# Attention products of two token tiles as one six-bank unit instead of one tile in four banks

## The chip, the cores and the metric

One core of a Trainium2 chip runs the whole kernel. The metric is the device time of one execution in microseconds, taken as the median of several executions. All executions used here were in the fast state, with the full clock granted to TensorE (0.999 to 1.0). Executions of one kernel scatter by about 0.5 us to either side.

The engines are named as the profile names them: PE is TensorE (PEld its weight loads), DVE is VectorE, ACT is ScalarE, POOL is GpSimd, SP is SyncE.

## The reference, cut to what matters

```python
# x: 1 x 2048 x 640, 32 heads of 20, F = 1536, bf16
xn = layernorm(x)
q, k, v = heads(xn @ wqkv)
phi_q = concat(softmax(q @ w_phi), softmax(-(q @ w_phi)))     # per head, 40 features
phi_k = concat(softmax(k @ w_phi), softmax(-(k @ w_phi)))
kv, z = einsum(phi_k, v), sum(phi_k)                          # over all tokens
o = (phi_q @ kv) / (phi_q @ z + 1e-6)
out = x + o @ wo + (silu(xn @ w1) * (xn @ w3)) @ w2
```

There are 16 token tiles of 128 tokens. The change concerns `phi_q @ kv` with its two denominators for each tile, and nothing else in the mathematics.

## The kernel before: the parts that matter

The kernel describes its work as units: a unit is a run of matmuls together with the PSUM banks that it fills (PSUM is the memory into which matmuls write) and the DVE and ACT operations that read them out. A list scheduler, which runs when the program is built, puts the units in an order on PE, gives each its banks out of eight, and orders the operations on every engine, from modelled durations. Near-ties are decided by pseudo-random tolerances drawn from `SEED`. So another seed gives another order of much the same instructions.

Four kinds of unit fill the second part of the program: Q units (`q_proj`, one bank, 5 matmuls of 512 columns, then two exponentials on ACT), gated units (`mlp`, two banks, 10 of 512), output units (`out_tile`, two banks, 34 of 320), and attention units:

```python
def q_tok(t, level):                      # one token tile; called 16 times
    u = P.begin(4, level, "row", "qt")    # four banks
    for sg in range(2):                   # exp(+) and exp(-)
        for c in range(DC):               # 5 groups of 4 heads (22 columns per head)
            for r in range(2):            # the two 64-row halves of the PE array
                j = 2 * sg + r
                mm(j, lambda k, j=j, c=c: bank(k + j, 88, 66 * c),
                   EqT[...][64 * r:64 * r + 64, sg, c, ...], KVc[64 * r:64 * r + 64, sg, c, :], ...)
    # ACT: two copies of the denominators out of PSUM into e_s, 64 each
    # DVE: pr = e * e', den = pr0 + pr1, 1/den, g = e' / den   (64, 32, 32, 64 elements)
    # DVE: prod = PSUM * g, 1280 elements, the last reader of all four banks
    # DVE: o = prod0 + prod1, then a DMA transpose into oT for the output unit
```

These matmuls contract over 64 rows, two of them side by side in the halves of the array; every other unit of this part uses the full 128 rows. So PE changes its mode on entering an attention unit and again on leaving it. The bank choice in the scheduler tries the places in order (cuts marked):

```python
for u in sorted(ready_u, key=lambda u: (-u.level, u.mms[0].idx)):
    ...
    for k in range(0, 8, u.banks) if u.anchor is None else ():
        ...
        g = group_time(u, k)              # when the banks' last readers are modelled to end
```

The program's first part, the front, normalises x, transposes it, computes K and V, and folds `w_phi` into the projections (units `fold0.0` to `fold0.4` make `Wqp`, the folded Q weights). It ends with a unit named `kvback`, which sets up `KVc`; the attention part follows.

The softmax here doesn't subtract the row's maximum and nothing guards it: scores larger than these inputs give would overflow.

Of the kernel before, what the change touches and what calls it, by code (L numbers as in the profile page):

```python
# [4 lines left out]
ACT = mybir.ActivationFunctionType  # L5
# [50 lines left out]
class _Unit:  # L56


    def __init__(self, banks, level, mode):
        self.banks, self.level, self.mode, self.k = banks, level, mode, None  # L60
        self.mms = []
        self.first = {}
        self.readers = [[] for _ in range(banks)]
        self.behind = []
        self.anchor = None
        self.name = ""


class _Program:
# [102 lines left out]
    def schedule(self, start, filler=None, filler_until=0.0, seed=None, shaken=0.0):  # L172
# [39 lines left out]
        mode = "full"  # L212
# [118 lines left out]

        def fit(k, n, t):

            if n == 4:
                return 0
            size = 2 * n
            base = k // size * size
            return sum(1 for i in range(base, base + size) if not k <= i < k + n and bank_time(i, 0.0, True) <= t)
# [3 lines left out]
        while left:  # L342
            best = None
            pick = None
            if ready_u:
# [7 lines left out]
                for u in sorted(ready_u, key=lambda u: (-u.level, u.mms[0].idx)):  # L353
                    opts = [(u.at, 0, u.anchor.k)] if u.anchor is not None else []
                    for k in range(0, 8, u.banks) if u.anchor is None else ():
                        if blocked & set(range(k, k + u.banks)):
                            continue
                        g = group_time(u, k)
                        if g < 1e8:
                            opts.append((max(g, u.at), fit(k, u.banks, u.at), k))  # L360
# [4 lines left out]
                    if u.banks == 4 and u.at <= t0 + 1.0 and not blocked and (not opts or x[0] > u.at + 0.03):  # L365
                        k = min((group_time(u, k, True), k) for k in (0, 4))[1]
                        blocked |= set(range(k, k + 4))
# [23 lines left out]
            if e == "PE":  # L391
# [25 lines left out]
                mode = x.mode  # L417
# [79 lines left out]
SEED = 1138  # L497
# [3 lines left out]
def bass_parallel_sum__linear_kernel_hedgehog__glu_gated_swiglu__prompt_kernel(  # L501
# [43 lines left out]
    pr_s = new("pr_s", [128, 2, 2, H], f32)  # L545
    den_s = new("den_s", [128, 2, H], f32)
    g_s = new("g_s", [128, 2, 2, H], f32)
# [37 lines left out]
    e_s = new("e_s", [128, 2, 4, H], f32, RV + 20480)  # L585
# [4 lines left out]
    prod = new("prod", [128, 2, 2, D], bf, RW + 1760)  # L590
# [411 lines left out]
    def q_tok(t, level):  # L1002
        b, jj = divmod(t, 4)
        u = P.begin(4, level, "row", "qt")
        u.name = f"qt{t}"
        u.behind.extend(turned[-1:])
        for sg in range(2):
            for c in range(DC):
                for r in range(2):
                    j = 2 * sg + r  # L1010
                    mm(j, lambda k, j=j, c=c: bank(k + j, 88, 66 * c),
                       EqT[b % 2][64 * r:64 * r + 64, sg, c, 128 * jj:128 * jj + 128],
                       KVc[64 * r:64 * r + 64, sg, c, :], c == 0, c == DC - 1, True,
                       0.003 if r == 0 else 0.045)

        def ps(k):
            a = PS[:, k * 512:(k + 4) * 512].rearrange("p (n c) -> p n c", c=512)[:, :, 0:352]
            return a.rearrange("p n (h c) -> p n h c", c=22)
        e = e_s[:, t % 2, :, :]
        up = 2e6  # L1020
        for sg in range(2):
            o = e[:, sg:4 - sg:3 - 2 * sg, :]
            add([w_act(o.rearrange("p c (q h) -> p q h c", h=16),
                       lambda k, sg=sg: ps(k)[:, 2 * sg:2 * sg + 2, :, 20:22], ACT.Copy, 64)],
                [e], [], [2 * sg, 2 * sg + 1], up)
        pr, den, g = pr_s[:, t % 2, :, :], den_s[:, t % 2, :], g_s[:, t % 2, :, :]
        add([w_tt("DVE", pr, e[:, 0:2, :], e[:, 2:4, :], ALU.mult, 64)], [pr], [e], None, up)
        add([w_tt("DVE", den, pr[:, 0, :], pr[:, 1, :], ALU.add, 32)], [den], [pr], None, up)
        add([w_op("DVE", "reciprocal", (den, den), 0.27, 0.36)], [den], [den], None, up)
        add([w_tt("DVE", g, e[:, 2:4, :], den.unsqueeze(1).to_broadcast([128, 2, 32]), ALU.mult, 64)],  # L1030
            [g], [e, den], None, up)
        gq = g.rearrange("p s (q h) -> p (s q) h", h=16)
        p2 = prod[:, t % 2, :, :]
        add([w_tt("DVE", p2.rearrange("p s (q h c) -> p (s q) h c", q=2, c=DH), lambda k: ps(k)[:, :, :, 0:DH],
                  gq.unsqueeze(3).to_broadcast([128, 4, 16, DH]), ALU.mult, 1280)],
            [p2], [g], [0, 1, 2, 3], up)
        turned.append(P.all[-1])
        o = o_tok[:, t % 4, :]
        add([w_tt("DVE", o, p2[:, 0, :], p2[:, 1, :], ALU.add, D, 2)], [o], [p2], None, 5e5)
        turn(oT[:, :, t * 128:(t + 1) * 128], o, 1e5 - t)  # L1040
# [21 lines left out]
    def out_tile(t, level):  # L1062
        b, ti = divmod(t, 4)
        u = P.begin(2, level, stream="O")
        u.name = f"O{t}"
        chunks = [(hT[b][:, i, ti * 128:(ti + 1) * 128], w2_s, i) for i in range(FC)]
# [139 lines left out]
    for b in range(NB):  # L1206
        for j in range(4):
            t = 4 * b + j
            q_tok(t, when(110 + t))
            if b + 1 < NB:  # L1210
                for fc in range((5 * j + 3) // 4, (5 * j + 8) // 4):
                    q_proj(b + 1, fc, when(110 + t + 0.1 * fc))
# [65 lines left out]
```

## Time and profile before

| | before |
|---|---|
| device time, median of 3 runs | 274.07 us (273.82 to 274.29) |
| span of the profiled execution | 271.7 us |
| DVE, ACT busy | 182.5 us, 101.8 us |
| from the first V matmul on the transposed tiles (`PS<-wv,xnT`) to the first matmul after `kvback` | 98.97 us |
| from there to the start of the last matmul | 157.92 us |

The span is the time between the first and last instruction of the profile; it is about 2 us shorter than the device time. The last two rows are differences of start times of matmuls in the trace. I shall call them the **middle** and the **attention part**. What lies ahead of the middle, some 12 us of loading and normalising the first token tiles and of early V matmuls on them, I call the **start**. Times between the starts of successive matmuls I call steps; a matmul is late by what its step is longer than usual for its shape. Some traces lack a few matmul records, and a step over a missing one is no wait. The lines of the page on which the argument stands are quoted in the prediction, those of a timeline with start in us, duration, engine, line, operation, operands, count. These are lines of the timeline of all engines before (start in us, duration, engine, line, operation, operands, count):

```profile
66.27 1.47 DVE L627 TENSOR_REDUCE S<-ekt 128x64 f32<-128x1280 bf16 x1
...
66.92 0.79 PE L619 MATMUL PS<-BDc,wqkT 128*128 128x140 bf16 x12
...
67.65 0.88 DVE L627 CAST Wqp<-PS 128x320 bf16<-128x320 f32 x2
68.31 0.77 ACT L627 ACTIVATE Wqp<-PS 128x320 bf16<-128x320 f32 x2
...
68.91 0.48 PE L619 MATMUL PS<-BDc,wqkT 128*128 128x140 bf16 x6
69.22 1.11 PE L619 MATMUL PS<-Wkp,xnT 128*128 128x320 bf16 x7
```

Two fold units (12 matmuls) start at 66.92. Behind a reduction (`S`) DVE makes two of the four copies that read them out of PSUM, until 68.53, and ACT the other two, until 69.08. The next fold unit, `fold0.3` (6 matmuls), starts at 68.91 and runs without a gap.

### The profile page before, as it was taken

How to read it: one execution, taken by the hardware profiler on the slowest of the kernel's cores; microseconds unless marked ns; L12 is line 12 of the kernel's file. 1: busy time of each engine (PE TensorE's matmuls, PEld its weight loads, DVE VectorE, ACT ScalarE, POOL GpSimd, SP SyncE). 2: the span in 40 equal slices, each digit the busy share in tenths (PEclk: the TensorE clock that was granted, in tenths of full speed). 3: DMA queues.
4: the chain of work that ended last, by engine and by line, in shares of the span. 5: the costliest groups of instructions: out<-in, count | busy, mean ns of one | idle time of the engine just before them, and what ended most of it. 6: DMA issues, size and time to landing. Idle time of an engine off the chain costs nothing.

```text
span 271.7 us, 5074 instructions
## 1 busy us (share of the span) xinstructions
PE 268.3 (99%) x2098; PEld 159.4 (59%) x2098; DVE 182.5 (67%) x325; ACT 101.8 (37%) x190; POOL 60.8 (22%) x101
## 2 busy tenths in 40 slices
PE   8999999999999999999999999999999999999996
PEld 5746546777754448444444446777677774444774
DVE  5758989999998453688869994777673215666112
ACT  6436726777744531355583354100100002222000
POOL 4320642789999900000000000000000000000000
PEclk9999999999999999999999999999999999999999
DMA  7657996763000001703041111333643122000001
GB/s 224 200 112 241 355 186 127 113 169 123 0 0 2 0 0 17 278 0 51 0 51 24 24 27 33 91 97 100 94 102 91 58 79 67 0 0 0 27 24 48
DMA packets 39975, 21.98 MB, mean 81 GB/s; under 512 B 27024, under 2 KB 39952, under 8 KB 39952
## 3 DMA queue, kind: packets, MB, share of 16 engines
q1 hardware_dynamic: 39376, 21.01, 31.8%
q10 hardware_dynamic: 576, 0.66, 0.7%
q8 instruction: 16, 0.26, 0.4%
q14 instruction: 7, 0.06, 0.1%
HBM read 12.81 MB, written 2.62 MB: 57 GB/s over the span
## 4 chain that ended last, share of the span: by engine, by line
PE 99%; DVE 0%; issue 0%
PE PS L619 96%; PE PS L1098 2%; PE PS L867 0%; PE PS L814 0%; DVE xres L627 0%
## 5 line engine op out<-in xcount | busy, mean ns | idle before, releaser
L619 PE MATMUL PS<-xnT,w_s 128*128 128x512 bf16 x480 | 106.6, 379 | 0.0
L619 PEld LDWEIGHTS PS<-xnT,w_s 128*128 128x128 bf16 x480 | 46.5, 98 | 54.7
L627 ACT ACTIVATE th<-PS 128x512 f32<-128x512 f32 x48 | 28.7, 597 | 71.9 <-PE PS L619 71.8
L619 PE MATMUL PS<-w_s,hT 128*128 128x320 bf16 (+2 forms) x384 | 55.0, 299 | 0.0
L627 DVE SCALAR_TENSOR_TENSOR t<-th,PS 128x512 bf16<-128x512 f32 x48 | 32.7, 683 | 27.5 <-ACT th L627 27.5
L619 PEld LDWEIGHTS PS<-w_s,hT 128*128 128x128 bf16 x384 | 37.0, 98 | 14.9
L627 POOL TENSOR_TENSOR ekt<-ekt,rS 128x640 bf16<-128x640 bf16 x32 | 39.4, 1269 | 1.1 <-DVE rS L627 1.1
L627 DVE TENSOR_TENSOR xres<-PS,xres 128x640 bf16<-128x640 f32 (+2 forms) x17 | 13.4, 786 | 37.8 <-PE PS L619 37.8
L627 DVE SCALAR_TENSOR_TENSOR hT<-t,PS 128x512 bf16<-128x512 bf16 x48 | 32.7, 684 | 1.3
L627 ACT ACTIVATE EqT<-PS 128x512 bf16<-128x512 f32 x40 | 21.9, 594 | 11.8 <-PE PS L619 11.7
L619 PE MATMUL PS<-wo_s,oT 128*128 128x320 bf16 (+2 forms) x160 | 24.5, 299 | 0.0
L627 DVE TENSOR_TENSOR prod<-PS,g_s 128x1280 bf16<-128x1280 f32 x16 | 23.9, 1491 | 0.6
L627 ACT ACTIVATE ekt<-PS 128x640 bf16<-128x640 f32 x32 | 20.8, 701 | 9.0 <-PE PS L619 8.8
L619 PE MATMUL PS<-Wkp,xnT 128*128 128x320 bf16 x160 | 23.9, 299 | 0.0
L619 PE MATMUL PS<-xnT,Wqp 128*128 128x512 bf16 x100 | 23.4, 380 | 0.0
L627 ACT ACTIVATE e_s<-PS 128x64 f32<-128x64 f32 x32 | 9.0, 283 | 38.2 <-PE PS L619 37.7
L627 DVE TENSOR_REDUCE S<-ekt 128x64 f32<-128x1280 bf16 x16 | 22.9, 1447 | 0.0
L619 PE MATMUL PS<-wv,xnT 128*128 128x320 bf16 x130 | 19.8, 299 | 0.0
L619 PEld LDWEIGHTS PS<-wo_s,oT 128*128 128x128 bf16 x160 | 15.7, 98 | 6.1
L619 PEld LDWEIGHTS PS<-Wkp,xnT 128*128 128x128 bf16 x160 | 15.5, 98 | 5.9
L619 PEld LDWEIGHTS PS<-xnT,Wqp 128*128 128x128 bf16 x100 | 9.4, 98 | 11.0
L627 DVE BATCH_NORM_STATS2 bst<-x_tok 128x6 f32<-128x320 bf16 x32 | 14.1, 469 | 2.4 <-DMA x_tok<-in_A_x_dram 2.4
(66 smaller groups left out, 163.3 us busy)
## 6 DMA issues: line engine op xcount, KB each, us to landing
w_s<-in_B_w_dram SPq DMA_DIRECT2D x6, 640.0 KB, 7.6
xres<-in_A_x_dram SPq DMA_DIRECT2D x16, 160.0 KB, 2.2
out_dram<-xres SPq DMA_DIRECT2D x15, 160.0 KB, 1.8
x_tok<-in_A_x_dram SPq DMA_DIRECT2D x3, 640.0 KB, 8.2
w_s<-in_B_w_dram SPq DMA_DIRECT2D x1, 1920.0 KB, 9.0
wo_s<-in_A_wo_dram SPq DMA_DIRECT2D x1, 800.0 KB, 4.8
x_tok<-in_A_x_dram SPq DMA_DIRECT2D x2, 160.0 KB, 3.4
x_tok<-in_A_x_dram ACTq DMA_DIRECT2D x2, 160.0 KB, 3.8
```

The lines of the kernel that those rows point to most:

```text
L619: return nc.tensor.matmul(o(u.k), l, r, start=start, stop=stop, skip_group_check=shared)
L627: return getattr(e, name)(*[at(a, u) for a in args], **{k: at(v, u) for k, v in kw.items()})
L1098: return nc.tensor.matmul(bank(u.k, n), ones[:, 0:128], ones[:, 0:n], start=True, stop=True)
```

## The change

The intent is to halve the number of mode changes: two tiles of attention run back to back in a unit of six banks. The small DVE and ACT operations are shared between the two tiles (128 or 64 elements at a time instead of 64 or 32), and the read-out product is split in three so that two banks at a time come free. As such a unit leaves only two banks to other work while it is read out, the scheduler is told to prefer a long output unit right behind it. The pseudo-random seed was chosen anew. The diff, cut to its core (cuts marked):

```diff
-                for u in sorted(ready_u, key=lambda u: (-u.level, u.mms[0].idx)):
+                for u in sorted(ready_u, key=lambda u: (-u.level - (1e7 if wide and u.long else 0), u.mms[0].idx)):
                     opts = [(u.at, 0, u.anchor.k)] if u.anchor is not None else []
-                    for k in range(0, 8, u.banks) if u.anchor is None else ():
+                    for k in places(u.banks) if u.anchor is None else ():
 ...
-SEED = 1138
+SEED = 61
 ...
     def q_tok(t, level):
         b, jj = divmod(t, 4)
-        u = P.begin(4, level, "row", "qt")
+        u = P.begin(6, level, "row", "qt")
 ...
         for sg in range(2):
-            for c in range(DC):
-                for r in range(2):
-                    j = 2 * sg + r
+            for m in range(2):
+                for c in range(DC):
+                    parts = ((0, 4),) if not sg or c != 2 else ((0, 1), (1, 4))
+                    for lo, hi in parts:
+                        for r in range(2):
+                            h = 3 * c + lo
+                            j, off = (4 + r, 256 * m + 22 * (h - 7)) if sg and h >= 7 else (2 * r + m, 22 * (16 * sg + h))
 ...
-        add([w_tt("DVE", p2..., lambda k: ps(k)[:, :, :, 0:DH], ..., ALU.mult, 1280)],
-            [p2], [g], [0, 1, 2, 3], up)
+        for r in range(2):
+            add([w_tt("DVE", o, lambda k, r=r: big(k)[:, 2 * r:2 * r + 2, :, 0:DH], ..., ALU.mult, 920)],
+                [o], [i], [2 * r, 2 * r + 1], up)
+        add([w_tt("DVE", o, lambda k: rest(k)[:, :, :, 0:DH], ..., ALU.mult, 720)], [o], [i], [4, 5], up)
 ...
     def out_tile(t, level):
+        u.long = True
 ...
-            q_tok(t, when(110 + t))
+            if j % 2 == 0:
+                q_tok(t, when(118 + 2.5 * t))
```

At one place per tile and sign, four heads straddle the end of a bank, and that matmul is split in one of 22 and one of 66 columns (`parts`).

More of the change, by code (lines that the diff above doesn't have):

```diff
@@ L65, in __init__ @@
         self.anchor = None
+        self.long = False
         self.name = ""
@@ L211, in schedule @@
         queues = {"SP": [], "ACT": []}
-        mode = "full"
+        mode, wide = "full", False
         owner = [None] * 8
@@ L330, in group_time, with places @@
             return max(bank_time(k + j, u.first[j].off if j in u.first else 0.0, guess) for j in range(u.banks))
+        def places(n):
+            return range(0, 9 - n, n if n < 4 else 8 - n)
         def fit(k, n, t):
-            if n == 4:
+            if n >= 4:
                 return 0
@@ L364, in schedule @@
                             pick = (x[0], u, x[2])
-                    if u.banks == 4 and u.at <= t0 + 1.0 and not blocked and (not opts or x[0] > u.at + 0.03):
-                        k = min((group_time(u, k, True), k) for k in (0, 4))[1]
-                        blocked |= set(range(k, k + 4))
+                    if u.banks >= 4 and u.at <= t0 + 1.0 and not blocked and (not opts or x[0] > u.at + 0.03):
+                        k = min((group_time(u, k, True), k) for k in places(u.banks))[1]
+                        blocked |= set(range(k, k + u.banks))
                 if pick is not None:
@@ L416, in schedule @@
                 x.k = k
-                mode = x.mode
+                mode, wide = x.mode, x.banks == 6
                 ready_u.remove(x)
@@ L544, in bass_parallel_sum__linear_kernel_hedgehog__glu_gated_swiglu__prompt_kernel @@
     warm = new("warm", [128, 8], f32)
-    pr_s = new("pr_s", [128, 2, 2, H], f32)
-    den_s = new("den_s", [128, 2, H], f32)
-    g_s = new("g_s", [128, 2, 2, H], f32)
+    pr_s = new("pr_s", [128, 2, 64], f32)
+    den_s = new("den_s", [128, 64], f32)
+    g_s = new("g_s", [128, 4, H], f32)
     S64 = new("S64", [128, 3, 64], f32)
@@ L584, in bass_parallel_sum__linear_kernel_hedgehog__glu_gated_swiglu__prompt_kernel @@
     oT = new("oT", [128, DC, S], bf, RV)
-    e_s = new("e_s", [128, 2, 4, H], f32, RV + 20480)
+    e_s = new("e_s", [128, 4, 64], f32, RV + 20480)
     RW = region(12800)
@@ L589, in bass_parallel_sum__linear_kernel_hedgehog__glu_gated_swiglu__prompt_kernel @@
     KVc = new("KVc", [128, 2, DC, 4 * 22], bf, RW)
-    prod = new("prod", [128, 2, 2, D], bf, RW + 1760)
+    prod = new("prod", [128, 4, H, DH], bf, RW + 1760)
     o_tok = new("o_tok", [128, 4, D], bf, RW + 6880)
@@ L1003, in q_tok @@
         b, jj = divmod(t, 4)
-        u = P.begin(4, level, "row", "qt")
+        u = P.begin(6, level, "row", "qt")
         u.name = f"qt{t}"
         u.behind.extend(turned[-1:])
+        seen = set()
         for sg in range(2):
-            for c in range(DC):
-                for r in range(2):
-                    j = 2 * sg + r
-                    mm(j, lambda k, j=j, c=c: bank(k + j, 88, 66 * c),
-                       EqT[b % 2][64 * r:64 * r + 64, sg, c, 128 * jj:128 * jj + 128],
-                       KVc[64 * r:64 * r + 64, sg, c, :], c == 0, c == DC - 1, True,
-                       0.003 if r == 0 else 0.045)
@@ L1016, in ps @@
-        def ps(k):
-            a = PS[:, k * 512:(k + 4) * 512].rearrange("p (n c) -> p n c", c=512)[:, :, 0:352]
+            for m in range(2):
[5 more added lines that the diff above has]
+                            j, off = (4 + r, 256 * m + 22 * (h - 7)) if sg and h >= 7 else (2 * r + m, 22 * (16 * sg + h))
+                            first = j not in seen
+                            seen.add(j)
+                            n = 22 * (hi - lo)
+                            mm(j, lambda k, j=j, n=n, off=off: bank(k + j, n, off),
+                               EqT[b % 2][64 * r:64 * r + 64, sg, c, 128 * (jj + m):128 * (jj + m) + 128],
+                               KVc[64 * r:64 * r + 64, sg, c, 22 * lo:22 * hi], first,
+                               sg == 1 and (c == 2 and hi == 1 if j < 4 else m == 1 and c == DC - 1), True,
+                               0.003 if r == 0 else max(0.026, 0.008 + n / 2400))
@@ L1018, in ps, with big, rest @@
+        def big(k):
+            a = PS[:, k * 512:(k + 4) * 512].rearrange("p (n c) -> p n c", c=512)[:, :, 0:506]
             return a.rearrange("p n (h c) -> p n h c", c=22)
-        e = e_s[:, t % 2, :, :]
+        def rest(k):
+            a = PS[:, (k + 4) * 512:(k + 6) * 512].rearrange("p (n c) -> p n c", c=256)[:, :, 0:198]
+            return a.rearrange("p n (h c) -> p n h c", c=22)
         up = 2e6
-        for sg in range(2):
-            o = e[:, sg:4 - sg:3 - 2 * sg, :]
-            add([w_act(o.rearrange("p c (q h) -> p q h c", h=16),
-                       lambda k, sg=sg: ps(k)[:, 2 * sg:2 * sg + 2, :, 20:22], ACT.Copy, 64)],
-                [e], [], [2 * sg, 2 * sg + 1], up)
@@ L1026, in q_tok @@
-        pr, den, g = pr_s[:, t % 2, :, :], den_s[:, t % 2, :], g_s[:, t % 2, :, :]
-        add([w_tt("DVE", pr, e[:, 0:2, :], e[:, 2:4, :], ALU.mult, 64)], [pr], [e], None, up)
-        add([w_tt("DVE", den, pr[:, 0, :], pr[:, 1, :], ALU.add, 32)], [den], [pr], None, up)
-        add([w_op("DVE", "reciprocal", (den, den), 0.27, 0.36)], [den], [den], None, up)
-        add([w_tt("DVE", g, e[:, 2:4, :], den.unsqueeze(1).to_broadcast([128, 2, 32]), ALU.mult, 64)],
-            [g], [e, den], None, up)
@@ L1032, in q_tok @@
-        gq = g.rearrange("p s (q h) -> p (s q) h", h=16)
-        p2 = prod[:, t % 2, :, :]
-        add([w_tt("DVE", p2.rearrange("p s (q h c) -> p (s q) h c", q=2, c=DH), lambda k: ps(k)[:, :, :, 0:DH],
-                  gq.unsqueeze(3).to_broadcast([128, 4, 16, DH]), ALU.mult, 1280)],
-            [p2], [g], [0, 1, 2, 3], up)
-        turned.append(P.all[-1])
-        o = o_tok[:, t % 4, :]
-        add([w_tt("DVE", o, p2[:, 0, :], p2[:, 1, :], ALU.add, D, 2)], [o], [p2], None, 5e5)
-        turn(oT[:, :, t * 128:(t + 1) * 128], o, 1e5 - t)
+        e = e_s[:].rearrange("p q (n h) -> p n h q", h=16)
@@ new lines, in q_tok @@
+        for src, o, js in ((lambda k: big(k)[:, :, 0:16, 20:22], e[:, :, :, 0:4:3], [0, 1, 2, 3]),
+                           (lambda k: big(k)[:, :, 16:23, 20:22], e[:, :, 0:7, 1:3], [0, 1, 2, 3]),
+                           (lambda k: rest(k)[:, :, :, 20:22], e[:, :, 7:16, 1:3], [4, 5])):
+            add([w_act(o, src, ACT.Copy, free(o))], [e_s[:]], [], js, up)
+        add([w_tt("DVE", pr_s[:], e_s[:, 0:2, :], e_s[:, 2:4, :], ALU.mult, 128)], [pr_s[:]], [e_s[:]], None, up)
+        add([w_tt("DVE", den_s[:], pr_s[:, 0, :], pr_s[:, 1, :], ALU.add, 64)], [den_s[:]], [pr_s[:]], None, up)
@@ new lines, in q_tok @@
+        add([w_op("DVE", "reciprocal", (den_s[:], den_s[:]), 0.47, 0.56)], [den_s[:]], [den_s[:]], None, up)
+        g = g_s[:].rearrange("p n (s h) -> p s n h", h=16)
+        for sg in range(2):
+            dn = den_s[:].rearrange("p (n h) -> p n h", h=16)
+            add([w_tt("DVE", g[:, sg, :, :], e_s[:, 2 + sg, :].rearrange("p (n h) -> p n h", h=16), dn, ALU.mult, 64)],
+                [g_s[:]], [e_s[:], den_s[:]], None, up)
+        for r in range(2):
+            o, i = prod[:, 2 * r:2 * r + 2, 0:23, :], g_s[:, 2 * r:2 * r + 2, 0:23]
+            add([w_tt("DVE", o, lambda k, r=r: big(k)[:, 2 * r:2 * r + 2, :, 0:DH],
+                      i.unsqueeze(3).to_broadcast([128, 2, 23, DH]), ALU.mult, 920)], [o], [i], [2 * r, 2 * r + 1], up)
@@ new lines, in q_tok @@
+        o, i = prod[:, :, 23:32, :], g_s[:, :, 23:32]
+        add([w_tt("DVE", o, lambda k: rest(k)[:, :, :, 0:DH], i.unsqueeze(3).to_broadcast([128, 4, 9, DH]), ALU.mult,
+                  720)], [o], [i], [4, 5], up)
+        turned.append(P.all[-1])
+        for m in range(2):
+            o = o_tok[:, (t + m) % 4, :]
+            i0, i1 = prod[:, m:4:2, 0:16, :], prod[:, m:4:2, 16:32, :]
+            add([w_tt("DVE", o.rearrange("p (r h c) -> p r h c", r=2, c=DH), i0, i1, ALU.add, D, 2)], [o], [i0, i1],
+                None, 5e5)
+            turn(oT[:, :, (t + m) * 128:(t + m + 1) * 128], o, 1e5 - t - m)
@@ L1208, in bass_parallel_sum__linear_kernel_hedgehog__glu_gated_swiglu__prompt_kernel @@
             t = 4 * b + j
-            q_tok(t, when(110 + t))
+            if j % 2 == 0:
+                q_tok(t, when(118 + 2.5 * t))
             if b + 1 < NB:
                 for fc in range((5 * j + 3) // 4, (5 * j + 8) // 4):
-                    q_proj(b + 1, fc, when(110 + t + 0.1 * fc))
+                    q_proj(b + 1, fc, when(118 + 2.5 * t + 0.1 * fc))
     for t in range(T):
```

## The prediction

> **What bounds the kernel now.** I read the page from the top (busy shares, then the chain that ended last), then the list of waits, then the timeline of TensorE alone, then the trace's start times matmul by matmul.
>
> ```profile
> PE 268.3 (99%) x2098; PEld 159.4 (59%) x2098; DVE 182.5 (67%) x325; ACT 101.8 (37%) x190; POOL 60.8 (22%) x101
> ```
> ```profile
> PE 99%; DVE 0%; issue 0%
> ```
>
> TensorE (PE) is busy for 268.3 of 271.7 us, and the chain is PE from end to end. VectorE and ScalarE have idle time, so making their work shorter gives nothing by itself. What can help is fewer or cheaper PE slots; what can hurt is a wait that PE does not have today. Busy does not mean efficient, so I looked at how far apart the matmuls start. The timeline of PE where output units (24 + 10 matmuls of 320 columns) alternate with attention units (20 of 88 columns), and further down where output units follow each other:
>
> ```profile
> 169.74 0.57 PE L619 MATMUL PS<-KVc,EqT 64*128 64x88 bf16 x20
> 170.24 3.43 PE L619 MATMUL PS<-w_s,hT 128*128 128x320 bf16 x24
> 173.51 1.52 PE L619 MATMUL PS<-wo_s,oT 128*128 128x320 bf16 x10
> 174.97 0.56 PE L619 MATMUL PS<-KVc,EqT 64*128 64x88 bf16 x20
> ...
> 206.20 3.42 PE L619 MATMUL PS<-w_s,hT 128*128 128x320 bf16 x24
> 209.46 1.52 PE L619 MATMUL PS<-wo_s,oT 128*128 128x320 bf16 x10
> 210.82 3.42 PE L619 MATMUL PS<-w_s,hT 128*128 128x320 bf16 x24
> ```
>
> An output unit alone repeats every 210.82 - 206.20 = 4.62 us, which is 34 steps of 136 ns. With an attention unit the period is 174.97 - 169.74 = 5.23 us. One attention unit therefore takes 0.60 us of PE. Single start times split it: the step into the unit is 231 ns where 136 would be normal (95 lost); the step out of it is 134 ns where an 88-column step of 39 would do (95 lost), and the next step is 146 instead of 136 (10 lost). That is 0.20 us for turning the array to 64 rows and back. The rest, 0.40 us, is ten pairs at about 39 ns, plus 8 ns at the start. All 16 units show the same figures, whatever unit stands next to them. From 118 us to the end no other matmul starts late by more than 8 ns: today there is no PSUM wait at all in this part.
>
> **What the Trainium skill says.** "TensorEngine Tiling (Array Packing)", Key Properties: "Mode switching requires drain: Changing tiling mode (not just tile) drains the TensorE". The trace agrees: 95 ns each way, now paid 32 times. "TensorE: Matmul & The Clock Gate", the section "Wait — 56ns, not 53.3ns?": warm matmuls start N/2.4 GHz + about 2.5 ns apart, and never under about 25 ns. The trace agrees (216 ns at 512 columns, 136 at 320, 39 per pair at 88). Its Part 3 says that matmuls in different row groups run together about 4 ns apart; the two halves of a pair start 3 to 4 ns apart here. "PSUM — Partial Sum Buffer", the section on bank collisions: the chip does not stall when an engine reads a bank that PE writes, it reports an error; so PE must wait for the readers, and six banks held by one unit leave two to work in. No wait of that kind is to be seen in this part before.
>
> **The change part by part.**
>
> (1) Removed: 16 attention units become 8, so 8 round trips of 0.20 us go, together with 8 of the 8-ns starts: 8 x 0.209 = 1.67 us.
>
> (2) Added on PE: four bank-crossing chunks are split per unit, giving 44 matmuls (22 pairs) instead of 40. A pair of 88 columns (39 ns) becomes one of 22 (about 27, at the floor) and one of 66 (about 30), twice a unit: 8 x 2 x 18 = 0.29 us. So a wide unit should take 1.03 us against 2 x 0.604. PE saves about 1.4 us before any waits.
>
> (3) VectorE and ScalarE. These rows give their sizes:
>
> ```profile
> L627 DVE TENSOR_TENSOR prod<-PS,g_s 128x1280 bf16<-128x1280 f32 x16 | 23.9, 1491 | 0.6
> L627 DVE RECIPROCAL den_s<-den_s 128x32 f32<-128x32 f32 x16 | 5.6, 353 | 0.5
> L627 DVE TENSOR_TENSOR g_s<-e_s,den_s 128x64 f32<-128x64 f32 x16 | 3.6, 225 | 0.6
> L627 ACT ACTIVATE e_s<-PS 128x64 f32<-128x64 f32 x32 | 9.0, 283 | 38.2 <-PE PS L619 37.7
> ```
>
> At 1.04 ns an element over a fixed 0.16 us, the product of 1280 becomes two of 920 (1.12 us) and one of 720 (0.91). The 64-wide reciprocal takes 0.54 (the same shape stands elsewhere at 536 ns). The DVE chain of a pair is about 4.6 us against 5.0 for two singles. ScalarE does three copies (0.9 us) instead of four (1.13). Neither engine limits, so I credit nothing.
>
> (4) Moved: what the banks allow. By the built program's order the wide units are followed by four Q projections (twice), an output unit (six times); each narrow follower has two banks. Counting from the start of a wide unit: it ends at 0.95, the copies at 2.0, four small DVE steps and the second gain product bring the first product to 3.75, and it ends at 4.87. An output unit holds PE until 5.57, so banks come free in time: **this ordering hides the long read-out**, with some 0.7 us to spare. But three short waits do come up.
> - Q projections in two banks. In the trace a Q unit takes 1.08 us of PE; its first exponential starts 0.416 us after its fifth matmul, the second ends 1.085 us later. Start to bank free is 0.873 + 0.416 + 1.085 = 2.37, plus 0.06 us from a releaser's end to the matmul (DVE to PE at 10.9 us in the trace). The bank is wanted again after 2 x 1.08 = 2.17: PE waits 0.26 us, at two places: 0.53 us.
> - The output unit after the fifth pair takes the bank of a Q unit that ended just before the pair; its exponentials end at 1.19, wanted at 1.10: 0.15 us.
> - Output units that take a bank whose last reader (hT or xres) ends at about 1.0 to 1.1: five places of 0.03, together 0.16 us.
> Sum of new waits: 0.84 us.
>
> (5) The front, to 103 us, and the end after the last pair run the same matmuls in almost the same order (another seed moves a few filler matmuls and copies). I take them as equal within 0.15 us.
>
> Sum: -1.67 + 0.29 + 0.84 = -0.54 us: 274.07 becomes 273.5.
>
> **The rivals.**
>
> (a) PE waits are smaller than I count: the scheduler placed the units so that banks fit, and my waits are sums of small margins. For it: output units leave 0.7 us of room. Then the full 1.4 us shows: 272.7.
>
> (b) The read-out of a wide unit becomes the bound: PE waits for DVE. Against it: DVE is 67% busy and falls. For it: between 120 and 165 us DVE also serves gated units, and the first product ends 4.87 us after the unit starts; if the chain were 1 us longer, eight units would wait 0.3 us or more each, and the gain is gone or turned: 274.5 to 276.
>
> (c) The narrow pairs cost more than their columns, because each needs two weight loads of its own: at 39 ns each the split costs 0.63 us instead of 0.29: 273.8.
>
> (d) The shared small operations are the gain. Against it: no PE wait ends on them today, and PE sets the time; I give this no microseconds.
>
> **Range and chances.** The largest possible gain is about 1.4 us, half a percent, since only mode turns are removed. For a 2% gain 5.5 us would have to go, more than the 3.2 us that all 16 turns cost. For a 2% loss each wide unit would have to wait 0.9 us more than saved. I choose 273.4 us, between my sum and rival (a), leaning to the sum. The range 272.6 to 274.3 holds (a) and (c) and a little of (b). Faster by over 2%: 0.01; within 2%: 0.97; slower: 0.02.
>
> **What would show it.** In the changed profile: PE still 99% of the chain; 352 attention matmuls in 8 bursts of about 0.9 us; entry and exit still about 95 ns late, 16 times instead of 32 (step 1); pairs of 22 and 66 columns starting some 27 and 30 ns apart (step 2); DVE busy some 2.5 us less (step 3); the third Q unit after the first and third pair starting about 0.26 us late on ScalarE, the second matmul of the output unit after the fifth pair about 0.15 us (step 4). The prediction is wrong if PE starts late behind product operations, if the front moves by over 0.3 us, or if the narrow pairs don't follow their columns.

## The result, and the profile after

Beside the changed kernel the kernel before took 273.94 us in the median of six runs; the changed one took 273.89 us (273.60 to 274.13). The ratio is 1.0001, with a 95% interval of 0.9988 to 1.0015. Ratios here are the mean time of one kernel's fast runs over that of the other's fast runs of the same rounds, so they are not quite the ratio of the medians quoted. In the later repeat (e8) the changed kernel took 273.72 us against 273.77, ratio 0.9994 [0.9979, 1.0010]. The change is worth nothing that the clock can tell.

The busy shares and the two lines of the chain of waits that ended last, after:

```profile
PE 267.7 (98%) x2128; PEld 159.3 (59%) x2128; DVE 179.9 (66%) x310; ACT 100.1 (37%) x181; POOL 61.1 (22%) x101
...
PE 83%; DVE 10%; DMA 2%; issue 2%; ACT 1%; POOL 1%; SPq 0%
PE PS L623 82%; DVE S L631 3%; DMA x_tok<-in_A_x_dram 2%; DVE x_tok L631 2%; DVE bst L631 1%; DVE rS L631 1%; POOL mv L631 1%; ACT EqT L631 1%; DVE hT L631 1%; DVE t L631 1%; DVE Wqp L631 0%; PE PS L871 0%; SPq L693 0%; DVE mv L631 0%; ACT th L631 0%
```

PE is busy for 0.6 us less, DVE for 2.6 us less. But a part of the chain has left PE: `S`, `x_tok`, `bst` and `rS` are all operations of the front. A share of 10% does not mean that DVE costs 10% of the time. The chain follows a releaser back through whatever was waiting on what, and one short wait of PE on DVE leads it along DVE's whole queue. What it does say is that somewhere in the front PE now waits for DVE, which it did not before.

The timeline of PE, after, where pairs and output units alternate:

```profile
195.18 3.42 PE L623 MATMUL PS<-w_s,hT 128*128 128x320 bf16 x24
198.44 1.52 PE L623 MATMUL PS<-wo_s,oT 128*128 128x320 bf16 x10
199.89 0.99 PE L623 MATMUL PS<-KVc,EqT 64*128 64x88 bf16 x44
200.88 3.43 PE L623 MATMUL PS<-w_s,hT 128*128 128x320 bf16 x24
204.15 1.52 PE L623 MATMUL PS<-wo_s,oT 128*128 128x320 bf16 x10
205.51 3.42 PE L623 MATMUL PS<-w_s,hT 128*128 128x320 bf16 x24
```

An output unit alone repeats after 4.63 us (205.51 - 200.88); with a pair ahead of it, the period is 200.88 - 195.18 = 5.70. Here one pair of tiles costs 1.07 us, where two single units cost 1.21; at the places without a wait behind the pair it is 1.03. The four row forms of the read-out, after (count, then busy us and mean ns, then idle time ahead of them):

```profile
L631 DVE TENSOR_TENSOR prod<-PS,g_s 128x920 bf16<-128x920 f32 x16 | 17.1, 1111 | 0.3
L631 DVE TENSOR_TENSOR prod<-PS,g_s 128x720 bf16<-128x720 f32 x8 | 7.2, 898 | 0.0
L631 DVE RECIPROCAL den_s<-den_s 128x64 f32<-128x64 f32 x8 | 4.4, 553 | 0.3
L631 ACT ACTIVATE e_s<-PS 128x128 f32<-128x128 f32 x8 | 3.2, 398 | 35.4 <-PE PS L623 35.4
```

They have the sizes that were predicted (1.12, 0.91 and 0.54 us for the first three), and the 35.4 us ahead of the ACT row is idle time of an engine that is not the bound.

Cutting the span by matmul start times tells where the time went. The last column is the sum of the three:

| us | start | middle | attention part | sum |
|---|---|---|---|---|
| before | 12.05 | 98.97 | 157.92 | 268.94 |
| after | 12.27 | 99.54 | 157.53 | 269.34 |
| difference | +0.22 | +0.57 | -0.39 | +0.40 |

In these two traces the attention part does gain 0.39 us, the middle loses 0.57, and the start another 0.22 (spans 271.7 and 272.1). Two questions follow. Is the loss in the front a result of the pairing, of the new seed, or of chance? And why does the attention part gain only 0.39 us when eight turns are saved?

For the second, the start times give the terms. Inside a pair unit, it is 0.921 us from the first attention matmul to the first matmul of the next unit (129.022 - 128.101 for the first pair), against 0.498 us in a single unit. With the 95 ns of turning in ahead of it and the 10 ns lost just behind it, the unit takes 0.095 + 0.921 + 0.010 = 1.026 us, against 2 x 0.604 before. Eight units save 8 x 0.182 = 1.46 us. Against this stand eight short waits: one Q unit 0.26 us late after the first pair and another after the third, an output unit 0.19 us late after the fifth pair, and five output units 0.06 to 0.07 us late, together 1.03 us. The net of these is -0.43 us, and -0.39 was measured. This is what the first of the two long waits looks like in the timeline of all engines, after:

```profile
129.18 1.03 ACT L631 ACTIVATE e_s<-PS 128x128 f32<-128x128 f32 x3
...
130.31 2.17 ACT L631 ACTIVATE EqT<-PS 128x512 bf16<-128x512 f32 x4
...
131.45 0.76 PEld L623 LDWEIGHTS PS<-xnT,Wqp 128*128 128x128 bf16 x5 [0.59 <-ACT EqT L631]
```

The third Q unit behind the pair has no third bank: six of eight are held by the pair. It must wait until ACT has finished both exponentials of the first Q unit, and ACT starts those after its three copies for the pair. The last exponential ends at 131.399 in the trace, and the matmul starts at 131.453. The 0.59 us in brackets is idle time of the weight loads; the matmul itself is 0.26 us later than its usual step.

And this is the wait in the front, timeline of all engines, after, at the place shown above for the kernel before:

```profile
67.11 0.79 PE L623 MATMUL PS<-BDc,wqkT 128*128 128x140 bf16 x12
67.12 1.47 DVE L631 TENSOR_REDUCE S<-ekt 128x64 f32<-128x1280 bf16 x1
...
68.49 0.45 ACT L631 ACTIVATE Wqp<-PS 128x320 bf16<-128x320 f32 x1
68.51 1.28 DVE L631 CAST Wqp<-PS 128x320 bf16<-128x320 f32 x3
...
69.09 0.32 PE L623 MATMUL PS<-BDc,wqkT 128*128 128x140 bf16 x3
...
69.84 0.33 PE L623 MATMUL PS<-BDc,wqkT 128*128 128x80 bf16 x3 [0.43 <-DVE Wqp L631]
```

In both kernels a reduction of 1.47 us (`S`) stands ahead of the `Wqp` copies in DVE's queue. With the new seed it starts together with the two fold units (67.12 against 67.11) where it started 0.65 us ahead of them before, and DVE makes three of the four copies where it made two. So the last copy ends 2.68 us after these units start (69.79 - 67.11), where it was 2.16 before (69.08 - 66.92). And unit `fold0.3` is given the very pair of banks that `fold0.2` has just filled (4 and 5); in the kernel before it was given another pair (0 and 1). The second half of `fold0.3` therefore waits for the copies that free the bank: by the usual step its 80-column matmul is 0.59 us late. (The bracket says 0.43 because the profile counts idle time from the modelled end of the matmul before.)

### The profile page after: what moved, and what is told of

It is laid out like the page before. It is cut to its first block, busy times and chain, and to the rows that moved or that the text cites. A ratio compares the mean times of both kernels' runs of the same rounds, so it can differ in the third digit from the quotient of the medians.

```text
span 272.1 us, 5108 instructions
## 1 busy us (share of the span) xinstructions
PE 267.7 (98%) x2128; PEld 159.3 (59%) x2128; DVE 179.9 (66%) x310; ACT 100.1 (37%) x181; POOL 61.1 (22%) x101
## 4 chain that ended last, share of the span: by engine, by line
PE 83%; DVE 10%; DMA 2%; issue 2%; ACT 1%; POOL 1%; SPq 0%
PE PS L623 82%; DVE S L631 3%; DMA x_tok<-in_A_x_dram 2%; DVE x_tok L631 2%; DVE bst L631 1%; DVE rS L631 1%; POOL mv L631 1%; ACT EqT L631 1%; DVE hT L631 1%; DVE t L631 1%; DVE Wqp L631 0%; PE PS L871 0%; SPq L693 0%; DVE mv L631 0%; ACT th L631 0%
## 5 line engine op out<-in xcount | busy, mean ns | idle before, releaser
L631 DVE TENSOR_TENSOR prod<-PS,g_s 128x920 bf16<-128x920 f32 (+1 forms) x24 | 23.6, 1040 | 0.3
L631 ACT ACTIVATE e_s<-PS 128x128 f32<-128x128 f32 (+2 forms) x24 | 7.7, 320 | 35.9 <-PE PS L623 35.4
```

Of the source, the lines that this page charges most:

```text
L631: return getattr(e, name)(*[at(a, u) for a in args], **{k: at(v, u) for k, v in kw.items()})
```

## The experiments

The theory, **T**: pairing saves some 1.4 us of PE, waits for banks in the attention part take most of that, and the new seed's order in the front, which has nothing to do with pairing, gives back the rest. Rivals: **R1**, the front's loss is chance of the run and pairing itself is worth nothing; **R2**, the small waits come from somewhere else, and the mode turns are worth less than counted; **R3**, what gain there is comes from the shorter DVE and ACT work. Eleven kernels ran, in four groups. Medians of the kernel before in the same groups were 273.77 (e1, e2, e8, e9), 273.77 (e3, e4, e5, e7), 273.76 (e6) and 273.75 us (e10, e11). All eleven kernels gave correct results.

### The two halves of the change apart: e1 and e2

To take the front from one seed and the attention part from another, the generator is started anew once `kvback` is placed. e1 is the changed kernel with the old front and the same attention order and banks as after; e2 is the kernel before with the new front and single tiles behind it.

```diff
# e1, from the kernel after            # e2, the same in the kernel before:
-SEED = 61                             # SEED = 61, SEED2 = 24
+SEED = 1138
+SEED2 = 13
 ...
+                if x.name == "kvback" and seed is not None:
+                    rng = random.Random(SEED2)
```

> The paired attention units in exactly the order and banks of the changed kernel, behind the front (everything up to the small kvback unit at 111 us) of the kernel before. Theory: the pairing is worth what the trace of the changed kernel shows after kvback (157.09 us against 157.48, so -0.39 us), and the seed's new front takes it back. Then 0.39 us under the kernel before, ratio about 0.9986. In the trace the new PE waits stay (0.26 us at the third Q unit after the first and third pair, 0.19 at the output unit after the fifth). Rival A: pairing is worth nothing and the front is the same; then ratio 1.000. Rival B: the 0.59 us and 0.22 us that the changed kernel's front lost are chance of one execution; then the time is that of the changed kernel.

Measured: 273.56 us, ratio 0.9984 [0.9966, 1.0001]. In its trace the middle is 98.97 us and the attention part 157.54.

> The reverse: attention units of the kernel before (16 single ones, another order among them but no PSUM wait planned), behind the front of the changed kernel. Theory: slower than the kernel before by what the new front costs, 0.4 to 0.8 us (ratio 1.0015 to 1.003), with PE waiting about 0.2 us longer near 8.5 us and 0.6 us near 69.8 us. Rivals A and B: as the kernel before, ratio 1.000.

Measured: 273.97 us, ratio 1.0005 [0.9990, 1.0019]; middle 99.56, attention part 157.92. Its list of waits (total us, count, longest) has the front's wait, with no pairs in the program:

```profile
PE PS L622 <- DVE Wqp L630: 0.4, 1, 0.4
```

By their times alone both runs are within the interval of no effect, and both say no more than which way they lean. The traces say more: the middle goes with the seed (98.97 with the old front in either kernel, 99.54 and 99.56 with the new, single or paired), and the attention part goes with the pairing (157.53 to 157.54 against 157.92), in every combination. R1 falls for the middle and for the attention part. It holds for the start: e1, with the old front, took 12.75 us there, e2, with the new, 11.74, the reverse of the pair before and after. Over the thirteen traces this part lay between 11.74 and 12.87 us and followed neither seed nor pairing. It goes with the loads of x: the fourth load of x landed at 7.12 to 7.36 us in the nine traces with a start of 12.23 or less, and at 7.81 to 8.16 in the four with a longer one. In the traces this is most of the scatter; that it is so in the executions without a trace too is likely, but not shown. So the expectations were missed where they spoke of the start: e2 has no longer wait of PE near 8.5 us.

### The changed kernel again: e8

> The changed kernel once more, for a second trace of its front. Theory (the front's order causes its waits): PE again waits about 0.56 us near 8.7 us and 0.59 us near 69.8 us; ratio 1.000 to 1.0015. Rival B (chance): one of these waits is gone or much smaller.

No edit. Measured: 273.72 us, ratio 0.9994 [0.9979, 1.0010]; start 12.28, middle 99.64, attention part 157.53. The wait in the front is there again (0.61 us). So it belongs to this order, not to one execution. The wait near 8.7 us is there too (0.54 us of idle time), but e2 and e10, which have the new front, don't show it, and e1, with the old one, has one of 0.61 us near 9.1 us: it goes with the start.

### What a mode turn costs: e3 and e4

e3 gives the kernel before one more turn in each of its 16 attention units, by a full-array matmul of 32 columns in the middle, whose result the following real matmul overwrites. e4 gives e1 one such turn in each of its 8 pairs, between the two tiles: as many turns as before the change.

```diff
 def emit():
+    if turn_here:
+        nc.tensor.matmul(bank(u.k + j, 32), ones[:, 0:128], ones[:, 0:32], start=True, stop=True)
     return nc.tensor.matmul(o(u.k), l, r, ...)
 # e3: turn_here = sg == 1 and c == 0 and r == 0
 # e4: turn_here = sg == 0 and m == 1 and c == 0 and r == 0
```

> The kernel before with one dummy matmul of the full array (32 columns) in the middle of each of the 16 attention units: 16 more round trips of the array's row mode, nothing else moved. Theory (a round trip costs 0.20 us of PE, as the trace of before shows at each unit): 16 x (0.20 + 0.025) = 3.6 us more, ratio about 1.013. Rival (the turns are hidden or cost only when other work is refilled): under 1 us more.

Measured: 277.22 us, ratio 1.0126 [1.0111, 1.0141]; attention part 161.58, that is +3.66 us or 0.229 a unit. The timeline of PE in e3 shows the unit cut in two with the added matmul between:

```profile
171.75 0.37 PE L621 MATMUL PS<-KVc,EqT 64*128 64x88 bf16 x10
172.06 0.19 PE L620 MATMUL PS<-const-bfloat16-1.0 128*128 128x32 bf16 x1
172.18 0.37 PE L621 MATMUL PS<-KVc,EqT 64*128 64x88 bf16 x10
172.48 3.43 PE L621 MATMUL PS<-w_s,hT 128*128 128x320 bf16 x24
```

> The pairs behind the old front, with one such dummy in the middle of each of the 8 paired units, which gives the saved turns back and keeps the shared small operations and the order. Theory: 8 x 0.225 = 1.8 us more than the pairs without it, so about 275.3 us and slower than the kernel before by 1.4 us. Rival (shared small operations or order are the gain): no slower than the kernel before.

Measured: 274.53 us, ratio 1.0028 [1.0013, 1.0043]; attention part 158.86. That is +1.33 us against e1, and **less than expected**. The trace shows why. Each pair unit is 0.225 us longer, which makes 1.8 us, but the bank of the output unit behind it has that much more time to come free, and the six small waits (0.19 + 2 x 0.061 + 3 x 0.066, together 0.5 us) are gone: 1.8 - 0.5 = 1.3. So these waits and the turns are two sides of one thing: a shorter attention unit means that the next unit asks for its bank sooner. With the turns given back, e4's attention part is 0.94 us longer than that of the kernel before. With as many turns as before, the splits, the two Q waits and the eight added matmuls make pairs a loss. So the turns are worth what was counted, and without them there is no gain. R2 falls.

### Without the rule that an output unit follows: e5

```diff
# e5, from e1
-sorted(ready_u, key=lambda u: (-u.level - (1e7 if wide and u.long else 0), u.mms[0].idx))
+sorted(ready_u, key=lambda u: (-u.level, u.mms[0].idx))
```

> The pairs behind the old front without the rule that an output unit follows a pair; units of the gated part and Q units follow the second to fourth pair instead. Theory: those followers run out of free banks while the pair's six are read, and PE waits: 0.5 to 1.5 us at each of two or three places, 1.5 to 2.5 us slower than the pairs with the rule. Rival (the rule is needless): same time.

Measured: 275.19 us, ratio 1.0055 [1.0040, 1.0070]; attention part 159.38, +1.85 us on e1. The timeline of PE in e5, at the two longest waits:

```profile
143.41 2.33 PE L626 MATMUL PS<-xnT,Wqp 128*128 128x512 bf16 x10 [0.57 <-DVE t L634]
...
155.50 1.68 PE L626 MATMUL PS<-xnT,w_s 128*128 128x512 bf16 x7 [1.18 <-ACT EqT L634]
```

By step times PE stands 0.73 us at the first and 1.34 us at the second. Gated and Q units of 1 to 2 us need their two banks read out by DVE or ACT each time, and two banks don't carry them. An output unit fills two banks over 4.6 us. So, in the one order that was tried, the rule is a necessary part of the change: pairs without it lose to the kernel before. Whether another seed would do without it was not tested.

### The shared small operations: e6 and e7

e6 and e7 put DVE work back into each pair: the first small product `pr_s` is computed once more, or four times more, between itself and its reader, without the scheduler knowing. The seed for the attention part was set anew (15 and 4), so that order and banks are those of e1.

```diff
         add([w_tt("DVE", pr_s[:], ...)], [pr_s[:]], [e_s[:]], None, up)
+        for _ in range(4):                # e6: range(1)
+            eng, (again, _, _) = w_tt("DVE", pr_s[:], e_s[:, 0:2, :], e_s[:, 2:4, :], ALU.mult, 128)
+            add([(eng, (again, 0.0, -0.04))], [pr_s[:]], [e_s[:]], None, up)
```

> As the run with four more DVE operations, but with one: banks come free about 0.33 us later, nearly the 0.37 us of DVE work that pairing saves. Theory: under the room of 0.52 us at the tightest pair, so no PE wait is added and the time is that of the pairs behind the old front, ratio about 0.9986 to the kernel before. Rival (the shared small DVE operations are part of the gain): 0.3 us at each pair, 2.6 us slower.

Measured: 273.71 us, ratio 1.0001 [0.9988, 1.0015]; attention part 157.53. With one repetition (some 0.33 us a pair) the attention part does not move. The ratio of the times, 1.0001, is above the 0.9986 expected, which lies just outside its interval; as e6's trace has the middle and the attention part of e1, I put this down to the scatter of the start. R3 falls: DVE time saved in the pair's chain is not what pays.

> The pairs behind the old front, the first DVE operation of each pair issued four more times (the same result, each behind the one before), so that banks come free about 1.30 us later. Theory: the followers leave 0.52 to 0.74 us of room at the eight pairs (5.1 us in sum), so PE waits about 8 x 1.30 - 5.1 = 5.3 us more: about 278.8 us. Rival (DVE is never near the limit): within 1 us of the pairs.

Measured: 279.25 us, ratio 1.0196 [1.0178, 1.0215]; attention part 163.07, +5.53 us on e1. The timeline of e7 shows the five products in one row, and its list of waits shows that PE now waits for the product `prod` once at each of the eight pairs:

```profile
189.85 1.59 DVE L634 TENSOR_TENSOR pr_s<-e_s 128x128 f32<-128x128 f32 x5 [1.15 <-ACT e_s L634]
...
PE PS L626 <- DVE prod L634: 4.4, 8, 0.7
```

The same row has 0.29 us when the product runs once, so the chain is 1.30 us longer. Matmul by matmul against e1, PE comes 0.57 to 0.78 us later at each of the eight pairs, 5.28 us together; another 0.18 us is lost inside the third pair, where the profile names no releaser. The eight waits, subtracted from 1.30, leave the room that the changed kernel has, and its own trace says the same: the first product ends 4.9 us after its unit starts, and the next unit that wants those banks comes 5.5 to 5.7 us after, leaving 0.5 to 0.7. A longer read-out costs nothing up to there and its full excess from there on.

### The front's wait alone: e10

Only the place of one unit is changed in the kernel after; no instruction changes its order on any engine, though two later units take other banks as a result.

```diff
-                    for k in places(u.banks) if u.anchor is None else ():
+                    for k in (0,) if u.name == "fold0.3" else places(u.banks) if u.anchor is None else ():
```

> The changed kernel with the fourth folding unit of the front (68.9 us) in another bank pair, as the kernel before had it; two following units move to other banks too, and no instruction changes its place on any engine. Theory (the middle part, from the first V matmul on xnT to the attention part, is 0.57 to 0.66 us longer in the three traces of the new front only because this unit waits for a copy of the bank pair that it takes over): that part falls from 99.54 to 98.97 us, the attention part stays 157.53, and the time is 0.4 us under the kernel before. Rival (the wait is the late DVE copy itself and comes back at the next unit): no change.

Measured: 273.67 us, ratio 1.0004 [0.9990, 1.0017]; middle 99.31, attention part 157.53. **The expectation was missed.** The wait of 0.6 us is gone where it was, but PE waits 0.205 us a little later, at 70.91, and 0.151 us at 77.60, so only 0.2 to 0.3 us of the 0.57 to 0.66 come back. The two new waits, 0.356 us together, are what is left (99.31 - 98.97 = 0.34). The list of waits puts the first of them down to the same kind of copy:

```profile
PEld PS L623 <- DVE Wqp L631: 0.2, 1, 0.2
```

The bank's place is thus shown to be a part of the cause, about half of it. The remaining 0.35 us goes with the rest of the new order in the front (e1, which has the old order, doesn't show it). The traces say what it is. At 70.91 `fold0.4` takes the banks of `fold0.3`, as it did in the kernel before; but DVE's copy of `fold0.3` ends at 70.85 where it ended at 69.92. At 77.60 a K unit takes the banks of a gated unit whose last reader on DVE (`hT`) ends at 77.54. So both waits are for late readers on DVE; putting these alone back in their old places was not tested.

### A version without most of the waits: e9 and e11

If T is right, a version with the old front, pairs and fewer bank waits must beat both kernels. Behind three of the pairs the output unit waits at its second matmul, because its matmuls alternate between two banks and the second one needs the second bank at once. (Behind the last three pairs it waits 0.066 us at its first matmul, which the edit can't change.) In e9 the first three matmuls go to the first bank and the next three to the second, before the alternation starts; the modelled pair step and the modelled turn are brought to the measured ones, and the unit order comes from another seed. e11 is the same kernel again.

```diff
# e9 and e11, from e1
-SEED2 = 13
+SEED2 = 288
-MODE = 0.085
+MODE = 0.1
-    0.003 if r == 0 else max(0.026, 0.008 + n / 2400)
+    0.003 if r == 0 else max(0.024, n / 2400)
-            for n, (l, w, i) in enumerate(chunks):
-                for q in range(2):
-                    mm(q, ...)
+            order = [(q, n) for q in range(2) for n in range(3)]
+            order += [(q, n) for n in range(3, len(chunks)) for q in range(2)]
+            for q, n in order:
+                l, w, i = chunks[n]
+                mm(q, ...)
```

> Old front, paired units, output units that begin with three chunks of one bank and three of the other, and an order of units in which only one Q unit meets a bank still being read. Theory: of the 0.97 us of PE waits in the changed kernel's attention part some 0.5 us go, so about 0.9 us under the kernel before, ratio about 0.9965. Rival A (pairing is worth nothing): 1.000.

Measured: 273.20 us, ratio 0.9975 [0.9957, 0.9994]; middle 98.97, attention part 156.95.

> The version with fewer PE waits once more, for a second interval against the kernel before. Theory: middle part 98.97, attention part 156.95 as in its first trace, against 98.97 and 157.92 before: 0.97 us less, ratio 0.9965, plus the chance of the first 12 us. Rival (its first result was luck of the start): 0.999 or above.

Measured: 272.51 us, ratio 0.9965 [0.9952, 0.9978]; middle 98.97, attention part 156.94. Its timeline of PE at a pair that is followed by an output unit:

```profile
147.97 0.99 PE L626 MATMUL PS<-KVc,EqT 64*128 64x88 bf16 x44
148.89 3.43 PE L626 MATMUL PS<-w_s,hT 128*128 128x320 bf16 x24
152.16 1.52 PE L626 MATMUL PS<-wo_s,oT 128*128 128x320 bf16 x10
```

The first 24 matmuls of the output unit last 3.43 us. After, at two of the three pairs where the second matmul waits, they last longer by that wait:

```profile
141.12 3.50 PE L623 MATMUL PS<-w_s,hT 128*128 128x320 bf16 x24
...
175.41 3.62 PE L623 MATMUL PS<-w_s,hT 128*128 128x320 bf16 x24
```

Of the 1.03 us of waits 0.46 are left (one of 0.26, which is a Q unit, and three of 0.065, which are those at a first matmul), and the attention part is 0.97 us shorter than before. Both runs have intervals below 1. This version is about 0.3% faster than the kernel before, and in the same group as e8 it took 273.20 us against that run's 273.72. By the traces it is ahead of the changed kernel by some 1.2 us in the middle and the attention part; the difference of 0.5 us by time is at the edge of the scatter. The difference from the kernel before is beyond its interval, and well below 2%. Which of the edits and the new order brought how much was not taken apart.

## Why the prediction was right, and where it was off

The time was predicted at 273.4 us with a range from 272.6 to 274.3, and 273.89 was measured, within 2% of before as expected. But the range held the 274.07 us of the kernel before too, so this number alone is no test: a gain of some 0.6 us was forecast, and side by side the two kernels differ by 0.05. What supports the prediction is its steps, one by one:

- **Step 1 (eight turns, 1.67 us) and step 2 (narrow pairs, 0.29 us)** held. Together they made 1.38 us; 1.46 was measured from the start times. A round trip is worth what was counted: e3 measured 0.229 us for one, which includes its own 32-column matmul. The pair behind one of 22 columns starts about 30 ns later and that behind one of 66 columns about 29, so rival (c) did not come up.
- **Step 3 (DVE and ACT, credited nothing)** held: DVE fell by 2.6 us where 2.5 was predicted, and e6 gave some of it back for no change of the time. Rival (d) is refuted.
- **Step 4 (new waits, 0.84 us)** held in place and kind, and was short in size: 1.03 us. The two Q waits were 0.26 us each, as worked out. The output unit behind the fifth pair waited 0.19 instead of 0.15, and the five small waits were 0.06 to 0.07 each instead of 0.03. The room behind an output unit was predicted at some 0.7 us and is 0.5 to 0.7 (e7). Rival (b) did not come up, and e7 shows how near it is. Rival (a) did not come up either.
- **Step 5 (front and end equal within 0.15 us)** is the step that failed. The end was equal, but the new seed's front cost 0.57 to 0.66 us in the middle, in all three traces that have it, with pairs or without. I took "another seed moves a few filler matmuls and copies" as harmless because the matmuls are the same. It moved one unit to the banks of the unit just ahead of it, and let the copies that free them end 0.5 us later (2.68 against 2.16 us after the units start). The prediction had named a front that moves by over 0.3 us as a sign that it is wrong, and for this step it is. The claim that PE would still be 99% of the chain failed with it: 83%.

So the sum of -0.54 us became -0.39 in the attention part and +0.6 in the middle, which is about +0.2 us; the measured ratios (1.0001 and 0.9994) hold that and no effect alike. The centre of the prediction was half a microsecond low mostly for this one reason. Two things stay open: whether the late readers on DVE are all of the half of the loss in the front that the bank does not explain (e10 names them, but no run moves them alone), and why the loads of x land up to a microsecond later in some executions.

## What to carry to other kernels

When PE is the bound and a change removes fixed costs from it, count the banks as well: work that gets shorter asks for its bank sooner, and part of the saving returns as waits of a few hundredths to a few tenths of a microsecond. Where a pseudo-random order comes with the change, compare the parts of the program that the change does not touch first, by start times of the same matmuls; and test the change with the old order there. Then look for the second matmul of a unit: if it can stay in the bank that is free already, it need not wait for the other. Here three such waits, 0.3 us together, were gone in e11, where an edit of this kind came with a new order; how much was the edit's is not shown.

## What the Trainium skill lacked or had wrong

- "TensorEngine Tiling (Array Packing)", Key Properties, says that a change of mode drains TensorE and gives no time. Here the step into 64-row matmuls was 95 ns longer, the step out 91 to 95 ns and the one behind it 10 ns, and an added round trip with its 32-column matmul cost 0.229 us (e3, 16 of them 3.66 us).
- "TensorE: Matmul & The Clock Gate", the section "Wait — 56ns, not 53.3ns?": it gives a floor of about 25 ns from start to start, and no figure for pairs in the two row halves. Here such pairs repeated after about 30 ns at 22 columns and 29 ns at 66 columns, so there the columns did not count.
- I found on no page the time from the end of an operation that frees a PSUM bank to the start of the matmul that waits for it. It was 54 ns here from ACT (131.399 to 131.453 us, after) and 57 ns from DVE (69.786 to 69.843 us, after).
